# A weight piece's shift set ahead of two masks, and a product group that takes its operand half by half: two reorderings at the seam between an SSD scan and an ELU feed-forward layer

## The chip, the cores and the metric

The kernel runs on one core of a Trainium2 chip. The core has a matrix engine (TensorE, PE; its weight loads are listed apart as PEld), three elementwise engines (VectorE or DVE, ScalarE or ACT, GpSimd or POOL) and DMA queues, here issued by SyncE (SP). Each engine works through its own list of instructions in order; semaphores make one wait for another. The metric is the device time of one execution in microseconds; of several executions the median is given.

## The reference

Four batches of eight heads go through a chunked Mamba-2 state-space scan over 768 tokens (head width 32, state width 16). The result, one row of 256 numbers per token, goes through a feed-forward layer with an ELU in the middle.

```python
for c in range(nc):                      # chunks of 32 tokens
    la = log_a[:, :, sl]; cum = np.cumsum(la, axis=-1)
    L = np.exp(cum[:, :, :, None] - cum[:, :, None, :]) * causal
    M = np.einsum('bhin,bhjn->bhij', Cc, Bc) * L
    y_intra = np.einsum('bhij,bhjd->bhid', M, xc)
    y_inter = np.einsum('bhin,bhnd->bhid', Cc, state) * np.exp(cum)[..., None]
    y[:, :, sl] = y_intra + y_inter
    state = decay_full * state + np.sum(Bx, axis=2)
...
x = attn_out.transpose(0, 2, 1, 3).reshape(B * S, H * D)   # (3072, 256)
h = x @ w_in                                               # (3072, 2048)
g = np.where(h > 0.0, h, np.exp(np.minimum(h, 0.0)) - 1.0)
return (g @ w_out).astype(np.float32)                      # (3072, 256)
```

The two weight matrices come as float64.

## The kernel before

**Blocks.** The 3072 tokens are twelve blocks of 256 (`BLK`), in chunks of 64. Block `n` first goes through the scan, then through the layer. The scan of a block makes decays `L`, turned copies of B and C (`bt`, `ct`), C masked by the parity of the head (`ctm`, `mask_heads`, L477: two VectorE instructions for block one), C scaled by the running decay (`cts`, `turn_exp`, L458, written in place over `ct`), scores `ps_g` (`scores`, L582, from `bt` and `ctm`), weighted scores `M` (`weigh`, L591, on VectorE, four per block), state sums `ps_st` (`sums`, L612), states (`states`: `S_new` on VectorE, L627 and L629, and `Sx` on GpSimd, L634), and at last the output: `across` (L660, from the states and `cts`) and `inside` (L678, from `M`), both into `ps_y`. `inside` works in two halves `t`: heads zero to three, then heads four to seven. Each half is copied into `yT[n // 2][:, t]`; for block one the first half is copied by ScalarE (L695), the second by VectorE (L693), three copies each.

**Weights.** They arrive as float64 words in pieces, and are made float32 in five steps: `w_abs` (ScalarE, L205), `w_low` (ScalarE, L214, or VectorE, L218), `w_sign` and `w_high_a` (VectorE, L224 and L232), `w_high_b`, a shift with an exclusive or (VectorE, L239), and `w_sum`, an integer add (GpSimd, L249). Pieces 0 to 7 are the eight column groups of `w_in`, so piece 3 is the fourth; its magnitude lies in PSUM, so L232 and L239 of it read PSUM.

**First layer.** `l1(n, i)` multiplies block `n` by column group `i` into one PSUM buffer of 2 x 256 columns: for each of two column halves `j`, two products (`k`, the two halves of the 256 features, that is heads zero to three and four to seven, the `t` above). In the profile every float32 product is two passes, so a group of four products is eight. `parts=2` splits the 256 tokens into two halves, so that a group is eight products of 128 columns. The ELU follows with a lag: ScalarE (L730 and L737), then a join on VectorE (L738), which frees the buffer. There are seven rotating PSUM buffers (`p_a`), shared with the scores and the turned tiles.

**The order around the change** is written out by hand, one call after the other, and each engine keeps that order. In the stretch of block one, VectorE gets the first two steps of piece 3, the two masks of C, the shift of piece 3, the scaled C, an ELU join, two `M`, the states, two more `M`. TensorE has `l1(0, 2)`, the scores and sums of block one, `l1(0, 3)` (which reads piece 3), `across` and `inside` of block one, two small transposes, and then a loop of twelve groups (L1159), which starts with `l1(1, 0)` and `l1(1, 1)`, both with `parts=2`. From there on groups of the first layer, products of the second (L885) and scans of later blocks alternate; later blocks use split words and longer products (L832, L981).

Of the kernel before, what the change touches and what calls it, by code (L numbers as in the profile page):

```python
# [17 lines left out]
P = 128  # L18
Q = 64
BLK = 2 * P  # L20
# [7 lines left out]
def high_word_as_f32(word):  # L28

    return float(np.uint32(word).view(np.float32))  # L30
# [3 lines left out]
def kernel(  # L34
# [27 lines left out]
    nc = tc.nc  # L62
# [8 lines left out]
    KC, MC = DM // P, DF // P  # L71
# [19 lines left out]
    def psum(shape, name):  # L91
        return p_a.tile(shape, F32, tag="a", name=name)
# [7 lines left out]
    for k in range(4):  # L100
        (nc.scalar if k % 2 else nc.sync).dma_start(
            out=la0[BH * k:BH * (k + 1)],
# [61 lines left out]
    w_in = [None] * (DF // CW)  # L164
# [14 lines left out]
    def w_load(i, parts=1):  # L179
        if i < len(pieces):  # L180
            w_raw[i] = big([P, 2, 2 * CW], U32, "w64")
            for part in range(parts):
                cols = slice(2 * CW * part // parts, 2 * CW * (part + 1) // parts)
                nc.sync.dma_start(out=w_raw[i][:, :, cols], in_=pieces[i][1][:, :, cols])  # L184
# [37 lines left out]
    def w_sign(i, cols=slice(None)):  # L222
        w_parts_of(i)
        nc.vector.tensor_scalar(  # L224
            out=w_sgn[i][:, :, cols], in0=w_words(i)[1][:, :, cols], scalar1=0x80000000,
            scalar2=None, op0=ALU.bitwise_and)

    def w_high_a(i, cols=slice(None)):
        mag = w_abs_of.get((i, cols.start), w_mag[i])[:, :, cols]


        nc.vector.tensor_scalar(  # L232
            out=mag.bitcast(F32), in0=mag.bitcast(F32),
            scalar1=high_word_as_f32(0x38000000), scalar2=high_word_as_f32(0x47EFFFFF),
            op0=ALU.max, op1=ALU.min)

    def w_high_b(i, cols=slice(None), ks=slice(None)):
        mag, sgn = w_mag[i][:, ks, cols], w_sgn[i][:, ks, cols]
        nc.vector.scalar_tensor_tensor(  # L239
            out=mag, in0=w_abs_of.get((i, cols.start), w_mag[i])[:, ks, cols], scalar=3, in1=sgn,  # L240
            op0=ALU.logical_shift_left, op1=ALU.bitwise_xor)
# [47 lines left out]
    for v in range(2):  # L289
        nc.gpsimd.affine_select(  # L290
            out=low16[Q * v:Q * v + Q], in_=low16[Q * v:Q * v + Q], pattern=[[1, Q]],
# [5 lines left out]
        out=hmask, in_=hmask, pattern=[[-N, NH]], compare_op=ALU.is_ge, fill=0.0,  # L297
        base=0, channel_multiplier=1)
    nc.gpsimd.affine_select(
        out=hmask, in_=hmask, pattern=[[N, NH]], compare_op=ALU.is_ge, fill=0.0,  # L300
# [8 lines left out]
        out=minus, in0=ident, scalar1=-1.0, scalar2=None, op0=ALU.mult)  # L309
# [60 lines left out]
    def write_flat_exp():  # L370
        nc.sync.dma_start(out=flat_exp, in_=F[:, 1].rearrange("r u i -> r (u i)"))
# [15 lines left out]
    yT = {}  # L387
# [84 lines left out]
    def mask_heads(n, eng=nc.vector):  # L472
        s = st[n]
        s["ctm"] = att.tile([P, 2, 2, P], F32, tag="ctm", name="ctm")
        if eng is nc.vector:
            for k in range(2):
                eng.tensor_scalar(  # L477
                    out=s["ctm"][:, :, k], in0=s["ct"], scalar1=hmask2[:, k:k + 1],
                    scalar2=None, op0=ALU.mult)
            return  # L480
        eng.tensor_tensor(
            out=s["ctm"], in0=s["ct"].unsqueeze(2).to_broadcast([P, 2, 2, P]),
            in1=hmask2.unsqueeze(1).unsqueeze(3).to_broadcast([P, 2, 2, P]), op=ALU.mult)
# [74 lines left out]
    def decay_of(n, h):  # L558
        L, row = st[n]["L"], rows_of(n).start + NG * h
        for u in range(2):  # L560
            nc.scalar.activation(
                L[:, h, u], L[:, h, u], ACT.Exp, bias=ncum[:, u, row:row + 1])
        if h % 4 == 3:
            for v in range(2):
                part = L[Q * v:Q * v + Q, h - 3:h + 1]
                nc.gpsimd.affine_select(
                    out=part, in_=part, pattern=[[0, 4], [0, 2], [1, Q]],
                    compare_op=ALU.is_ge, fill=0.0, base=0, channel_multiplier=-1)
# [3 lines left out]
    def scores(*ns, pool=p_a, tag="a"):  # L572

        gs = [psum([P, len(ns), 2, 2, Q], "ps_g") for _ in range(3)]
        gs.append(pool.tile([P, len(ns), 2, 2, Q], F32, tag=tag, name="ps_g"))
        for at, n in enumerate(ns):
            s = st[n]
            for u in range(2):
                for v in range(2):
                    for q in range(4):  # L580
                        rows, toks = slice(32 * q, 32 * q + 32), slice(Q * v, Q * v + Q)
                        nc.tensor.matmul(  # L582
                            out=gs[q][toks, at, u], lhsT=s["bt"][rows, u, toks],
                            rhs=s["ctm"][rows, u, :, toks], start=True, stop=True,
                            tile_position=(32 * q, Q * v), skip_group_check=True)
            s["g"], s["M"] = [g[:, at] for g in gs], []

    def weigh(n, q):
        s = st[n]
        M = att.tile([P, 2, 2, Q], F32, tag="M", name="M", bufs=8)  # L590
        nc.vector.tensor_tensor(  # L591
            out=M, in0=s["g"][q],
            in1=s["L"][:, 2 * q:2 * q + 2].rearrange("p k u i -> p u k i"), op=ALU.mult)
        s["M"].append(M)
# [8 lines left out]
    def sums(*ns, pool=p_a, tag="a", parts=(None, None)):  # L603

        ps = [psum([P, len(ns), 2, 2 * D], "ps_st"),
              pool.tile([P, len(ns), 2, 2 * D], F32, tag=tag, name="ps_st")]
        for at, n in enumerate(ns):
            s = st[n]
            for u, v in chunks(n, parts[at] or whole):
                toks = slice(Q * v, Q * v + Q)  # L610
                for q in range(4):
                    nc.tensor.matmul(  # L612
                        out=ps[v][32 * q:32 * q + 32, at, u],
                        lhsT=s["sc"][toks, u, 2 * q:2 * q + 2].rearrange("p h n -> p (h n)"),
                        rhs=s["x"][toks, u, 2 * D * q:2 * D * (q + 1)], start=True, stop=True,
                        tile_position=(Q * v, 32 * q), skip_group_check=True)
            s["st"] = [p[:, at] for p in ps]
# [88 lines left out]
            g_of[n // 2, i] = big([P, 2, 2, BLK], F32, "g")  # L706
        return g_of[n // 2, i]

    def l1(n, i, parts=1):

        ps = psum([P, 2, BLK], "ps_h")
        for j in range(2):
            m = 2 * i + j
            for part in range(parts):
                toks = slice(part * BLK // parts, (part + 1) * BLK // parts)
                for k in range(KC):
                    nc.tensor.matmul(  # L717
                        out=ps[:, j, toks], lhsT=w_in[i][:, k, j * P:(j + 1) * P],
                        rhs=yT[n // 2][:, k, n % 2].rearrange("p u i -> p (u i)")[:, toks],
                        start=(k == 0), stop=(k == KC - 1))  # L720
        lag.append((n, i, ps))

    lag = []
# [308 lines left out]
    def w_take(i, low):  # L1032

        w_abs(i)
        w_low(i, low)
        w_sign(i)

    def w_give(i):

        w_high(i)  # L1040
        w_sum(i)
# [75 lines left out]
    w_low(3, nc.scalar)  # L1117
    w_sign(3)
    w_high_a(3)
    mask_heads(1)  # L1120
    w_high_b(3)
    write_flat_exp()
    load_bc(2)
    w_load(6)
# [34 lines left out]
    for s, (n, i) in enumerate((  # L1159
            (1, 0), (1, 1), (1, 2), (0, 4), (1, 3), (0, 5), (1, 4), (0, 6), (1, 5), (0, 7),  # L1160
            (1, 6), (1, 7))):
        l1(n, i, parts=2 if s < 2 else 1)
        if s < 8:
            decay_of(2, s)
        if s == 7:
            st[0] = kept
            scores(2)
            sums(2, 0, pool=p_o, tag="o", parts=(None, last))
            weigh(2, 0)
            weigh(2, 1)  # L1170
        if s % 2 == 1 and todo < 11:
            w_take(todo, nc.vector)
            w_give(todo)
            w_load(todo + 6)
            todo += 1
        if s in (1, 3):
            load_bc(3, us=(s // 2,))
        if s == 9:
            write_flat(0)
        if s == 4:  # L1180
            scaled(2, nc.gpsimd)
        if s == 5:
            turn(2)
            turn_exp(2)
        if s == 4:
            load_x(3)
            spread_exp(3)
        if s == 8:
            weigh(2, 2)
            weigh(2, 3)  # L1190
            states(0, last)
            st.pop(0)
            states(2)
        if s == 9:
            decay(3, 0)
            decay(3, 1)
        if s == 10:
            spread_cum(4)
            inside(across(2), 2)
        if len(lag) > 1:  # L1200
            elu()
# [23 lines left out]
    for j in range(2 * DIRECT):  # L1225
        n, i = 2 + j // DIRECT, j % DIRECT
# [47 lines left out]
    for j in range(8, 16):  # L1274
        i = j - 8
# [84 lines left out]
    for n in range(4, NP, 2):  # L1360
        m = n + 2 if n + 2 < NP else None
# [78 lines left out]
    n = NP - 2  # L1440
# [45 lines left out]
```

## Time and profile before

| | |
|---|---|
| median of 3 runs | 339.98 us (339.45 to 340.72) |
| profiled execution | 338.85 us |
| its span, first to last instruction | 337.1 us |
| busy: PE, DVE, ACT, POOL | 330.4, 286.7, 259.0, 214.2 us |
| share of PE in the chain that ended last | 92% |
| granted TensorE clock | 0.999 |

A row of the timeline gives the start in us from the beginning of the span, the duration, the engine, the line of the kernel, the operation, the tile written and those read, the shapes, and how many instructions are merged into the row (`x2`); in square brackets stands how long the engine had been idle before and what released it. A row of the table by stage gives the stage, its length, the busy time of PE, PEld, DVE, ACT and POOL with the instructions in brackets, the granted clock, and the DMA's share and rate. A row of waits gives who waited for whom, for how many us in all, how often, and the longest.

### The profile page before, as it was taken

The page shows a single profiled execution, that of the slowest core. Times are in us where ns is not written, and L with a number is a line of the kernel's source. Part 1 is how long each engine was busy: PE and PEld are TensorE (multiplying, and loading weights), DVE is VectorE, ACT ScalarE, POOL GpSimd, SP SyncE. Part 2 cuts the span into 40 slices and gives each one's busy share as a digit, 9 for nine tenths or more (in the row PEclk, how much of TensorE's full clock was granted, in tenths as well). Part 3 has the DMA queues.
Part 4 walks back from the last instruction along what each step waited for, and adds up shares of the span by engine and source line. Part 5 has one row for each costly group of instructions (what it writes and reads, how often), then busy time and mean ns, then how long its engine had stood idle before and what let it go on. Part 6 is the DMA issues. An engine that isn't in the chain of part 4 may idle for free.

```text
span 337.1 us, 9647 instructions
## 1 busy us (share of the span) xinstructions
PE 330.4 (98%) x3742; PEld 288.2 (85%) x3742; DVE 286.7 (85%) x511; ACT 259.0 (77%) x537; POOL 214.2 (64%) x242
## 2 busy tenths in 40 slices
PE   8899999999999999999999999999999999999995
PEld 5578888888888888888899988889889899999995
DVE  4998998889897889898989998989996978997942
ACT  5789989599857699857898866898867789897501
POOL 5454554648979396989489979388974355776000
PEclk9999999999999999999999999999999999999999
DMA  8889999553487388671769491669440762330101
GB/s 141 218 237 181 293 193 277 127 108 123 158 158 290 126 217 272 200 185 16 272 189 215 138 300 27 263 188 191 126 156 8 277 212 101 104 118 0 33 0 63
DMA packets 82956, 54.79 MB, mean 163 GB/s; under 512 B 59038, under 2 KB 68574, under 8 KB 82910
## 3 DMA queue, kind: packets, MB, share of 16 engines
q1 hardware_dynamic: 80734, 53.98, 57.4%
q8 instruction: 29, 0.48, 0.6%
q10 hardware_dynamic: 2176, 0.20, 0.5%
q14 instruction: 17, 0.14, 0.1%
HBM read 44.53 MB, written 9.63 MB: 161 GB/s over the span
## 4 chain that ended last, share of the span: by engine, by line
PE 92%; SPq 2%; DMA 2%; ACT 2%; DVE 1%; issue 0%; DVEq 0%; ACTq 0%
PE ps_o L981 24%; PE ps_h L832 20%; PE ps_o L885 12%; PE ps_h L717 11%; PE ps_w L832 10%; PE ps_both L981 6%; PE ps_y L678 3%; DMA w<-in_moe_w_in_dram 2%; PE ps_g L582 2%; PE ps_y L660 2%; PE ps_st L612 1%; PE ps_high L981 1%; SPq L156 1%; SPq L184 0%; ACT w_in L214 0%; SPq L124 0%
## 5 line engine op out<-in xcount | busy, mean ns | idle before, releaser
L899 POOL TENSOR_TENSOR g_words<-g_words,g_low 128x512 fp32r<-128x512 f32 x62 | 82.3, 1331 | 49.2 <-DVE g_low L923 25.8
L981 PE MATMUL ps_o<-o_words,g_words 128*128 128x256 f32 x448 | 83.4, 284 | 0.0
L981 PEld LDWEIGHTS ps_o<-o_words,g_words 128*128 128x128 f32 x448 | 72.9, 190 | 5.8 <-POOL g_words L899 0.8
L860 ACT ACTIVATE e<-ps_h 128x512 f32<-128x512 f32 x72 | 43.0, 597 | 35.1 <-DVE ps_h L848 35.1
L867 DVE SCALAR_TENSOR_TENSOR g<-e,ps_h 128x512 f32<-128x512 f32 x72 | 49.3, 684 | 19.0 <-ACT e L861 17.1
L981 PE MATMUL ps_o<-o_low,g_low 128*128 128x256 f32 x224 | 63.3, 283 | 0.0
L923 DVE SCALAR_TENSOR_TENSOR g_low<-g_words,g 128x512 fp32r<-128x512 f32 x72 | 63.3, 885 | 0.0
L848 DVE SCALAR_TENSOR_TENSOR ps_h<-ps_h,e 128x512 f32<-128x512 f32 x72 | 49.8, 691 | 2.7 <-ACT e L840 2.6
L832 PE MATMUL ps_w<-y_both,w_words 128*128 128x512 f32 x144 | 48.7, 419 | 0.0
L861 ACT ACTIVATE e<-e 128x512 f32<-128x512 f32 x72 | 45.5, 633 | 2.3
L717 PE MATMUL ps_h<-yT,w_in 128*128 128x256 f32 (+1 forms) x208 | 45.2, 367 | 1.6 <-ACT yT L695 1.0
L840 ACT ACTIVATE e<-ps_w 128x512 f32<-128x512 f32 x72 | 41.9, 582 | 5.4 <-PE ps_w L832 5.4
L885 PE MATMUL ps_o<-w_out,g 128*128 128x256 f32 x192 | 45.5, 380 | 0.0
L832 PE MATMUL ps_h<-y,w_words 128*128 128x512 f32 x144 | 45.3, 395 | 0.0
L832 PE MATMUL ps_h<-y,w 128*128 128x512 f32 x144 | 44.7, 391 | 0.0
L922 ACT ACTIVATE g_words<-g 128x512 fp32r<-128x512 f32 x72 | 43.6, 625 | 0.0
L981 PEld LDWEIGHTS ps_o<-o_low,g_low 128*128 128x128 f32 x224 | 42.7, 191 | 0.0
L717 PEld LDWEIGHTS ps_h<-yT,w_in 128*128 128x128 f32 x208 | 36.2, 190 | 7.5 <-POOL w_in L249 2.3
L885 PEld LDWEIGHTS ps_o<-w_out,g 128*128 128x128 f32 x192 | 36.1, 190 | 5.4
L832 PEld LDWEIGHTS ps_h<-y,w 128*128 128x128 f32 x144 | 27.0, 188 | 6.2
L832 PEld LDWEIGHTS ps_h<-y,w_words 128*128 128x128 f32 x144 | 26.6, 188 | 6.6 <-issue 0.7
L832 PEld LDWEIGHTS ps_w<-y_both,w_words 128*128 128x128 f32 x144 | 23.5, 191 | 2.0 <-ACT e L860 0.2
(132 smaller groups left out, 548.2 us busy)
## 6 DMA issues: line engine op xcount, KB each, us to landing
w_words<-w_kept SPq DMA_DIRECT2D x28, 512.0 KB
w<-w_kept SPq DMA_DIRECT2D x28, 256.0 KB
L<-flat SPq DMA_DIRECT2D x20, 256.0 KB
w<-in_moe_w_out_dram SPq DMA_DIRECT2D x8, 512.0 KB
w_kept<-w_words SPq DMA_DIRECT2D x8, 512.0 KB
w<-in_moe_w_in_dram SPq DMA_DIRECT2D x7, 512.0 KB
xr<-in_x_dram SPq DMA_DIRECT2D x24, 128.0 KB
out_dram<-eo SPq DMA_DIRECT2D x18, 128.0 KB
```

The costliest lines, as they stand in the source:

```text
L717: nc.tensor.matmul(out=ps[:, j, toks], lhsT=w_in[i][:, k, j * P:(j + 1) * P], rhs=yT[n // 2][:, k, n % 2].rearrange("p u i -> p (u i)")[:, ...
L832: nc.tensor.matmul(out=ps, lhsT=lhs[:, k], rhs=rhs[:, k], start=k == 0 and lhs is not w0, stop=k == KC - 1 and lhs is not w1)
L840: nc.scalar.activation(e, both, ACT.Copy, scale=WORD)
L848: nc.vector.scalar_tensor_tensor(out=high, in0=high, scalar=WORD - 1.0, in1=e, op0=ALU.mult, op1=ALU.add)
L860: nc.scalar.activation(e, high, ACT.Relu, scale=-1.0)
L861: nc.scalar.activation(e, e, ACT.Exp, scale=-1.0)
L867: nc.vector.scalar_tensor_tensor(out=g_tile(n, m // 2)[:, m % 2].rearrange("p b i -> p (b i)"), in0=e, scalar=1.0, in1=h, op0=ALU.subtract ...
L885: nc.tensor.matmul(out=o_of[n][:, ts], lhsT=g_of[n // 2, j][:, m % 2, n % 2, ts * P:(ts + 1) * P], rhs=w_out[j][:, m % 2], start=(m == 0 a ...
L899: nc.gpsimd.tensor_tensor(out=out, in0=in0, in1=in1, op=ALU.subtract)
L922: yield nc.scalar.activation(words[:, 0], g, ACT.Copy, scale=NEAR / WORD)
L923: yield nc.vector.scalar_tensor_tensor(out=low, in0=words[:, 0].bitcast(F32), scalar=WORD, in1=g, op0=ALU.mult, op1=ALU.subtract)
L981: nc.tensor.matmul(out=ps, lhsT=lhs, rhs=rhs, start=lhs is both_g and first > 0 or lhs is g1 and first > 1, stop=last and lhs is not g1, s ...
```

## The change

Two things move. First, the shift of piece 3 (`w_high_b(3)`) is issued ahead of `mask_heads(1)`, so that on VectorE it passes the two masks. Second, `l1` loses its split by tokens. The loop's first group, `l1(1, 0)`, now runs over the feature halves outside and the column halves inside: both column halves with heads zero to three, then both with heads four to seven, 256 tokens each; only its first product starts the PSUM buffer afresh. The second group, `l1(1, 1)`, becomes a group as all others, four products of 256 columns.

```diff
-    def l1(n, i, parts=1):
+    def l1(n, i, by_half=False):
         ps = psum([P, 2, BLK], "ps_h")
-        for j in range(2):
-            m = 2 * i + j
-            for part in range(parts):
-                toks = slice(part * BLK // parts, (part + 1) * BLK // parts)
-                for k in range(KC):
-                    nc.tensor.matmul(
-                        out=ps[:, j, toks], lhsT=w_in[i][:, k, j * P:(j + 1) * P],
-                        rhs=yT[n // 2][:, k, n % 2].rearrange("p u i -> p (u i)")[:, toks],
-                        start=(k == 0), stop=(k == KC - 1))
+        order = [(j, k) for j in range(2) for k in range(KC)]
+        if by_half:
+            order = [(j, k) for k in range(KC) for j in range(2)]
+        for at, (j, k) in enumerate(order):
+            nc.tensor.matmul(
+                out=ps[:, j], lhsT=w_in[i][:, k, j * P:(j + 1) * P],
+                rhs=yT[n // 2][:, k, n % 2].rearrange("p u i -> p (u i)"),
+                start=(at == 0 if by_half else k == 0), stop=(k == KC - 1),
+                skip_group_check=by_half)
         lag.append((n, i, ps))
...
     w_high_a(3)
+    w_high_b(3)
     mask_heads(1)
-    w_high_b(3)
     write_flat_exp()
...
-        l1(n, i, parts=2 if s < 2 else 1)
+        l1(n, i, by_half=s == 0)
```

## The prediction

> **What bounds the kernel now.** I read the page first, then the chain of waits, the table by stage, the waits inside the stage that the diff touches, and last the timeline of that stage engine by engine. Page, busy time and the chain that ended last:
>
> ```profile
> span 337.1 us, 9647 instructions
> PE 330.4 (98%) x3742; PEld 288.2 (85%) x3742; DVE 286.7 (85%) x511; ACT 259.0 (77%) x537; POOL 214.2 (64%) x242
> PE 92%; SPq 2%; DMA 2%; ACT 2%; DVE 1%; issue 0%; DVEq 0%; ACTq 0%
> ```
>
> TensorE (PE) is 98% busy and 92% of the chain. The table by stage shows where it is not full:
>
> ```profile
> 20.00:27.00 7.00, 6.45 (x172) 4.71 (x172) 6.52 (x19) 5.31 (x12) 2.50 (x5) 1.00 0.78 195
> 27.00:100.00 73.00, 73.00 (x801) 62.23 (x803) 64.69 (x129) 61.20 (x153) 45.70 (x60) 1.00 0.73 180
> 100.00:300.00 200.00, 199.81 (x2184) 176.59 (x2182) 176.85 (x290) 163.08 (x309) 146.78 (x142) 1.00 0.59 178
> ```
>
> After each stage's length comes PE's busy time: 6.45 of 7.00 us in the stage of the change, 73.00 of 73 and 199.81 of 200 behind it. So whatever moves the first product behind 27 us moves the end by the same amount, in either direction; nothing behind absorbs it. Both edits lie in that one stage. Its waits, and its timeline:
>
> ```profile
> PE ps_h L717 <- DVE M L591: 0.4, 1, 0.4
> PEld ps_h L717 <- DVE yT L693: 0.3, 1, 0.3
> ```
>
> ```profile
> 19.02 0.69 DVE L232 TENSOR_SCALAR ps_mag<-ps_mag 128x512 f32<-128x512 f32 x1
> 19.62 0.60 DVE L477 TENSOR_SCALAR ctm<-bct,hmask 128x256 f32<-128x256 f32 x2
> 20.14 0.68 DVE L239 SCALAR_TENSOR_TENSOR mag<-ps_mag,mag 128x512 uint32<-128x512 uint32 x1
> 20.74 0.41 DVE L458 TENSOR_TENSOR bct<-bct,ec 128x256 f32<-128x256 f32 x1
> 20.79 0.76 PE L582 MATMUL ps_g<-ctm,bct 32*64 32x128 f32 x32
> 20.96 1.33 POOL L249 TENSOR_TENSOR w_in<-mag,w_in 128x512 uint32<-128x512 uint32 x1 [1.39 <-DVE mag L239]
> 21.32 0.69 DVE L738 SCALAR_TENSOR_TENSOR g<-e,ps_h 128x512 f32<-128x512 f32 x1 [0.17 <-ACT e L737]
> 21.93 0.75 DVE L591 TENSOR_TENSOR M<-ps_g,L 128x256 f32<-128x256 f32 x2
> ```
>
> The reader is to see the order on VectorE (DVE): both masks, the shift of the fourth piece (L239), the scaled C (L458), the ELU join (L738), the first two M. GpSimd (POOL) sums the piece (L249) once the shift is done. The group l1(0, 3) starts at 22.35, when both its piece (20.96 + 1.33 = 22.29) and its PSUM buffer (first M, 21.93 + 0.42 = 22.35) have come: two releasers within 0.06 us.
>
> **Edit 1: the shift ahead of the masks.** No instruction is added or removed; on DVE the shift passes the two masks, no queue of DMAs is passed, and the rows on the other engines keep their order. Step by step:
>
> Masks before the shift now separate L232 from L239, which reads what L232 wrote. Next to each other they can't overlap. Unrelated neighbours overlap by 0.07 to 0.08 us (19.02 + 0.69 = 19.71 against 19.62); where the later one reads the earlier one's result the row is 16.25 + 0.42 = 16.67, next start 16.70, so 0.03. Shift: 19.74 to 20.42. First mask: 20.34, 0.34 long, to 20.68; the second issues at 20.60.
>
> The sum on POOL started 0.14 after the shift's end (20.82 to 20.96), so it now starts at 20.56 and lasts 1.28 us: to 21.84, 0.45 earlier. That gain is worth nothing by itself, because the M still frees the buffer at 22.35.
>
> But the sum now runs beside the second mask and L458; before, it began when both masks were done. What a POOL operation does to such DVE instructions, other stages show:
>
> ```profile
> 17.54 1.28 POOL L249 TENSOR_TENSOR w_in<-mag,w_in 128x512 uint32<-128x512 uint32 x1 [1.25 <-DVE mag L239]
> 17.98 1.12 DVE L224 TENSOR_SCALAR mag<-w 128x512 uint32<-128x512 uint32 x1
> 80.42 1.73 POOL L899 TENSOR_TENSOR w<-w_in,w_words 128x256 fp32r<-128x256 f32 x2
> 81.40 0.91 DVE L477 TENSOR_SCALAR ctm<-bct,hmask 128x256 f32<-128x256 f32 x1
> 82.11 0.71 POOL L566 TENSOR_SCALAR_AFFINE_SELECT L<-L 64x512 f32<-64x512 f32 x1
> 82.23 0.75 DVE L477 TENSOR_SCALAR ctm<-bct,hmask 128x256 f32<-128x256 f32 x1
> ```
>
> L224 is 0.42 us elsewhere; here it took 1.12 and ended 0.28 behind the sum. The same masks, of another block, took 0.91 and 0.75 instead of 0.34, and each ended 0.16 behind a POOL instruction (80.42 + 1.73 = 82.15, mask end 82.31; 82.82, mask end 82.98). DVE waits out the whole POOL instruction. PSUM readers don't: L232 kept 0.69 to 0.70 us beside sums.
>
> The price is bounded from both sides. None, if the second mask and L458 slip through: 0. Full, if the second mask waits: it ends at 21.84 + 0.15 = 21.99; L458 rewrites in place what the mask read, so it starts at 22.02 and ends at 22.43; L738 at 22.35 (its exponential is there since 21.29) to 23.04; first M 22.96 to 23.38; l1(0, 3) at 23.38 instead of 22.35: +1.03 us. The scores need both masks and go from 20.79 to 22.02; with the sums they last 1.16 us, to 23.18, inside that. Should the second mask win the 0.04 us race against the sum (20.60 against 20.56), L458 waits instead: its two inputs are in SBUF, and such a form (the words of w, 0.68 us alone) took 0.98 beside POOL in the row at 77.77. It then ends about 0.28 behind a sum that itself is put off by about 0.25 us, at 22.37, and l1(0, 3) starts near 23.32: +0.97. The race decides little. I take +1.03: the mask rows at 81.40 and 82.23 are the same instruction in the same shape, and in both the POOL instruction went first, at 82.11 with a lead of only 0.12 us.
>
> Here a page of the Trainium skill can be weighed. The first mask issues 0.22 us before the sum, as L458 did before (20.74 and 20.96), and that sum took 1.33 instead of 1.28 us. By SBUF — State Buffer, "Who interferes with whom", whichever issues first holds the shared ports for its whole instruction and the other fully blocks; then the sum would wait for the first mask's end (20.68, 0.12 us), and edit 1 would cost 1.15 instead of 1.03. The row of 1.33 shows 0.05 lost, so I stay with the rows.
>
> Later work of the stage moves as a whole: states, Sx, across and inside of block one hang on the same DVE order (Sx ended at 24.27 and across began at 24.27), so l1(1, 0) would start at 26.06 + 1.03 = 27.09.
>
> **Edit 2: l1(1, 0) by heads, whole tokens.** Before, the first products:
>
> ```profile
> 26.06 0.38 PE L717 MATMUL ps_h<-yT,w_in 128*128 128x128 f32 x1
> 26.28 0.28 PE L717 MATMUL ps_h<-yT,w_in 128*128 128x128 f32 x1
> 26.70 0.38 PE L717 MATMUL ps_h<-yT,w_in 128*128 128x128 f32 x1
> 30.15 0.38 PE L717 MATMUL ps_h<-yT,w_in 128*128 128x256 f32 x1
> ```
>
> A float32 product shows as two passes. Two passes on heads zero to three start at 26.06, then PE waits for the last DVE copy of heads four to seven (released 26.64), and groups (1, 0) and (1, 1) give way to the next at 30.15: 4.09 us for 32 passes of 128 columns. After: 16 passes of 256. A group of eight is 1.73 us in the chain (61.30 to 63.03), and 1.83 when it starts after a stop (22.35, second pass 22.67, then six more by 0.216 and the last one's own 0.216). So 1.83 + 1.73 = 3.56, a gain of 0.53 us. The cover: the first four passes last 0.32 + 3 x 0.216 = 0.97, to 27.03 on the old clock, and the copies are there at 26.64, 0.39 early. Were that cover gone, the stop would be back at up to 0.42. Of the gain about 0.11 is the halves themselves (32 x 0.1115 = 3.57 against 16 x 0.216 = 3.46). Behind it the fifth piece is ready at 28.78 and needed by (0, 4) only at 31.9: no new wait there, even 1 us later.
>
> **Sum.** +1.03 - 0.53 = +0.50 us. The profiled execution took 338.85 us for a span of 337.1, and would take 339.35; it lies 1.13 under the median shown, 339.98, which becomes 340.48. 0.5% (1.70 us) is about what a measurement of this kernel can tell from no change; this is 0.15%.
>
> **Rivals.** (a) No collision: the sum and the second mask don't get in each other's way. Then scores start near 21.0, done well before L591 needs them, l1(0, 3) stays at 22.35, and only edit 2 counts: 339.98 - 0.53 = 339.45. For it: which of POOL and mask goes first hangs on 0.04 us of estimate, and L224 at 12.88, issued 0.07 us ahead of a sum, kept its 0.42. Against: L458 must get through as well, and no row of the trace shows such a DVE instruction, issued behind a POOL instruction, ending before it. 0.15.
>
> (b) Edit 2 doesn't do what it says in time: the collision comes, and the copies of heads four to seven, which are behind more DVE work than the ScalarE copies, come so late that the wait is back. For it: DVE carries the whole delay; against: both halves of yT shift together, with 0.39 to spare. +1.03 - 0.11, about 340.9. 0.06.
>
> (c) The other side, clearly slower: the longer stops take PE's clock down. PE would rest from 20.86 to 22.02 and 0.2 us more before 23.38. If the granted clock halved from the stop to l1(1, 0) at 27.09, 6.2 us at half speed cost up to 3.1 more: 343.6. It decides from 2.4 us of half clock on (0.50 + 1.2 = 1.70). Against: a stop of 0.97 us ahead of 12.46 left the granted clock at 1.00 in every stage. By TensorE: Matmul & The Clock Gate, Part 1, the clock falls only after an idle window of about 3.4 us, which would exclude it; no run here shows such a window. 0.04.
>
> **How the numbers follow.** Forecast 0.72, (a) 0.15, (b) 0.06, (c) 0.04, unnamed 0.03. The prediction is 340.5. Single runs spread from 339.45 to 340.72, so a median may be off by 0.3: from (a) less 0.3, 339.1, to (b) with 0.4, 341.3. The forecast, (a) and (b) are all within 0.5%: same 0.93; (c) and part of the unnamed are slower, 0.05; faster 0.02, unnamed alone.
>
> **What would show it.** Right: in the changed profile the second mask takes about 1.4 us and ends just behind L249, L582 starts near 22.0, l1(0, 3) near 23.4, and the rows of l1(1, 0) follow each other without the stop at 26.28 to 26.70. Wrong: both masks at 0.34 and L458 at 0.41 (then (a)), a wait for DVE yT in front of the third product (then (b)), or a granted clock under 1.00 between 20 and 28 us (then (c)).

## The result, and the profile after

The changed kernel takes 342.57 us (median of nine executions, 341.39 to 345.15) against 339.59 us for the one before (nine, 338.94 to 340.72): ratio 1.0091, 95% interval 1.0067 to 1.0116. It is slower by 3.0 us, where 0.5 us was forecast and 341.3 us was the upper end of the range. The profiled execution took 342.11 us for a span of 340.4 us.

Page of the changed kernel, busy time and chain:

```profile
span 340.4 us, 9615 instructions
PE 330.6 (97%) x3726; PEld 287.5 (84%) x3726; DVE 288.0 (85%) x511; ACT 259.0 (76%) x537; POOL 214.6 (63%) x242
PE 92%; SPq 3%; DMA 2%; DVE 1%; issue 1%; DVEq 0%
```

PE has the same busy time in a span that is 3.3 us longer, and 16 entries fewer in each of its two rows. So the loss is made of stops. The table by stage, of the changed kernel, shows where (length of the stage, then PE's busy time):

```profile
20.00:27.00 7.00, 5.38 (x131) 3.86 (x130) 6.61 (x17) 4.32 (x9) 2.45 (x6) 1.00 0.87 208
100.00:155.00 55.00, 55.00 (x570) 46.93 (x570) 47.20 (x76) 43.54 (x83) 44.71 (x46) 1.00 0.68 209
155.00:162.00 7.00, 5.72 (x200) 5.10 (x199) 5.03 (x6) 4.67 (x10) 6.31 (x5) 1.00 0.11 16
```

There are two places: the stage of the change, and one at 155 to 162 us, 130 us behind it, where PE was busy for 6.81 us before. In the first, the collision of edit 1 came as described. Timeline of the changed kernel, VectorE and GpSimd, with the two masks also one by one:

```profile
20.19 0.69 DVE L239 SCALAR_TENSOR_TENSOR mag<-ps_mag,mag 128x512 uint32<-128x512 uint32 x1
20.79 0.34 DVE L477 TENSOR_SCALAR ctm<-bct,hmask 128x256 f32<-128x256 f32 x1
21.02 1.26 POOL L249 TENSOR_TENSOR w_in<-mag,w_in 128x512 uint32<-128x512 uint32 x1 [1.00 <-DVE mag L239]
21.05 1.38 DVE L477 TENSOR_SCALAR ctm<-bct,hmask 128x256 f32<-128x256 f32 x1
22.54 0.42 DVE L458 TENSOR_TENSOR bct<-bct,ec 128x256 f32<-128x256 f32 x1
22.58 0.70 PE L582 MATMUL ps_g<-ctm,bct 32*64 32x128 f32 x32 [1.27 <-DVE ctm L477]
```

The second mask is issued 0.03 us behind the sum, takes 1.38 us instead of 0.34 and ends at 22.43, 0.15 behind the sum's end. Then comes what the prediction had not: rows of PE for the output of block one and, later, of blocks four and five, in the changed kernel:

```profile
26.22 0.44 PE L678 MATMUL ps_y<-M,xr 64*32 64x64 f32 x28
27.34 0.60 PE L678 MATMUL ps_y<-M,xr 64*32 64x64 f32 x36 [0.68 <-issue]
158.16 1.29 PE L678 MATMUL ps_y<-M,xr 64*32 64x64 f32 x104
160.72 0.43 PE L678 MATMUL ps_y<-M,xr 64*32 64x64 f32 x24 [1.28 <-issue]
```

In the middle of a run of small products PE stands still, and the profile names no engine or DMA as releaser ("issue"). Before, the second of these places had 0.19 us, the first none:

```profile
157.68 0.65 PE L678 MATMUL ps_y<-M,xr 64*32 64x64 f32 x40 [0.19 <-issue]
```

Setting the two traces side by side, product by product, gives the delay of the changed kernel against before. It is +0.40 us ahead of the stage (the start-up differs by up to 1.5 us from one profile to the next, in unchanged code), +1.36 at l1(0, 3), +2.19 at l1(1, 0), +1.67 at the transposes behind the sixth group, +1.75 at 147 us, +2.82 behind the stop near 160 us, +3.16 at 248 us. So: collision +0.96, stop in block one +0.83 with what surrounds it, edit 2 -0.52, stop in blocks four and five +1.07, and about 0.3 in small pieces behind.

### The profile page after: what moved, and what is told of

It reads as the page before. It is cut to its first block, busy times and chain, and to the rows that moved or that the text cites. A ratio compares the mean times of both kernels' runs of the same rounds, so it can differ in the third digit from the quotient of the medians.

```text
span 340.4 us, 9615 instructions
## 1 busy us (share of the span) xinstructions
PE 330.6 (97%) x3726; PEld 287.5 (84%) x3726; DVE 288.0 (85%) x511; ACT 259.0 (76%) x537; POOL 214.6 (63%) x242
## 4 chain that ended last, share of the span: by engine, by line
PE 92%; SPq 3%; DMA 2%; DVE 1%; issue 1%; DVEq 0%
PE ps_o L981 24%; PE ps_h L832 20%; PE ps_o L885 12%; PE ps_h L716 11%; PE ps_w L832 10%; PE ps_both L981 6%; PE ps_y L678 3%; PE ps_g L582 2%; DMA w<-in_moe_w_in_dram 2%; PE ps_y L660 2%; PE ps_st L612 1%; SPq L140 1%; PE ps_high L981 1%; SPq L184 1%; SPq L156 1%
## 5 line engine op out<-in xcount | busy, mean ns | idle before, releaser
L832 PE MATMUL ps_w<-y_both,w_words 128*128 128x512 f32 x144 | 48.6, 419 | 0.0
L716 PE MATMUL ps_h<-yT,w_in 128*128 128x256 f32 x192 | 44.9, 383 | 1.2 <-ACT yT L695 1.0
L832 PE MATMUL ps_h<-y,w_words 128*128 128x512 f32 x144 | 45.3, 395 | 0.0
L832 PE MATMUL ps_h<-y,w 128*128 128x512 f32 x144 | 44.6, 391 | 0.0
L716 PEld LDWEIGHTS ps_h<-yT,w_in 128*128 128x128 f32 x192 | 35.6, 190 | 7.3 <-POOL w_in L249 2.1
L832 PEld LDWEIGHTS ps_h<-y,w_words 128*128 128x128 f32 x144 | 26.6, 188 | 6.8 <-issue 0.5
L832 PEld LDWEIGHTS ps_h<-y,w 128*128 128x128 f32 x144 | 27.0, 188 | 6.2
L832 PEld LDWEIGHTS ps_w<-y_both,w_words 128*128 128x128 f32 x144 | 23.6, 191 | 1.9 <-DVE y_both L816 0.2
```

Source lines behind the costliest of these rows:

```text
L716: nc.tensor.matmul(out=ps[:, j], lhsT=w_in[i][:, k, j * P:(j + 1) * P], rhs=yT[n // 2][:, k, n % 2].rearrange("p u i -> p (u i)"), start=( ...
L832: nc.tensor.matmul(out=ps, lhsT=lhs[:, k], rhs=rhs[:, k], start=k == 0 and lhs is not w0, stop=k == KC - 1 and lhs is not w1)
```

## Experiments: collision, or also the two stops, and where these come from

Each run below is set against executions of the kernel before in the same round, so that the time before reads 339.45 to 339.68 us. The ratio in brackets, with its 95% interval, is not quite that of the two medians (for edit 2 alone these give 1.0052, where the ratio is 1.0045), so a few tenths of a us between two runs are not to be read.

A theory had to explain stops without a releaser. The page lists a DMA queue of its own for instructions, here in the changed kernel:

```profile
q8 instruction: 29, 0.48, 0.6%
```

0.48 MB in 29 packets are 16,384 bytes each. Counting PE's entries in the trace in order (products, weight loads and what its sequencer handles alone; 7584 before, 7552 after), the two stops of the changed kernel fall at entries 961 and 4033, which lie exactly 12 x 256 apart, and the stop of before falls at 4033 too. So the theory ("code theory"): PE's list of instructions arrives in blocks of 256; PE stops at a border if it has run through a block faster than the next was fetched. Small products run through one in less than 2 us (entries 3777 to 4033 of the changed kernel pass in 1.64 us). A group in whole tokens has four products instead of eight; a float32 product is four entries, so edit 2 takes 32 entries out and moves all later borders. The rival ("delay theory"): the stops follow from the later start of everything, by new collisions of transfers.

The Trainium skill, Runtime: NRT & Kernel Launch, "Instruction fetch mechanics", describes such blocks of 16 KiB and 256 instructions, fetched while the one ahead is executed, and calls the cost mostly hidden. The 16,384 bytes and the distance of 256 agree. It is hidden at most borders here too (in the kernel before, the stop of 0.19 us is PE's only one behind 27 us), but not at all: at two borders PE of the changed kernel stops for 0.68 and 1.28 us.

### Each edit alone, and the count alone

Edit 1 alone:

```diff
     w_high_a(3)
+    w_high_b(3)
     mask_heads(1)
-    w_high_b(3)
```

> Edit 1 alone (shift of piece 3 ahead of the masks; products as before). Code theory: besides the collision on GpSimd's sum, the extra loss comes from blocks of PE's instruction list that arrive late; their borders lie where PE's instruction count puts them. Then this run, which keeps PE's count, loses the collision (+1.0 us at l1(0, 3)) and perhaps the stop inside block one's L678 (+0.7 to 0.9, because the block needed there is asked for only when the scores start, now beside the loads of block two), in all +1.0 to +2.0 us, and shows no stop near 157 to 161 us longer than the 0.19 us of before. Delay theory: everything beyond the collision follows from the later start of the rest, whatever the count: +3.0 (result) + 0.5 (gain of edit 2 missing) = +3.5 us, with a stop of 1.2 us or more near 160 us.

Measured: 341.05 us against 339.68, +1.4 us (ratio 1.0046, 1.0028 to 1.0065). The second mask took 1.39 us. PE stopped in block one, and the place near 157 us had no stop:

```profile
27.53 0.60 PE L678 MATMUL ps_y<-M,xr 64*32 64x64 f32 x36 [0.60 <-issue]
```

The delay theory's +3.5 us fails, although everything behind started late.

Edit 2 alone:

```diff
-        l1(n, i, parts=2 if s < 2 else 1)
+        l1(n, i, by_half=s == 0)
```

> Edit 2 alone (masks first, as before; l1(1, 0) by heads, whole tokens in both groups). Code theory: -0.5 us at the group behind l1(1, 1), then a stop of 1.0 to 1.5 us inside L678 near 157 to 160 us and some 0.2 to 0.3 us near 245 us, since eight products fewer move the borders of the instruction blocks: in all +0.4 to +1.0 us. Delay theory: no late start, so no stop: -0.5 us (-0.3 to -0.7). No collision: both masks at 0.34 us.

Measured: 341.45 us against 339.68, +1.8 us (1.0045, 1.0025 to 1.0064), more than either theory said; the direction is that of the code theory. Both masks took 0.34 us, nothing was late, and still:

```profile
156.19 1.29 PE L678 MATMUL ps_y<-M,xr 64*32 64x64 f32 x104
159.12 0.43 PE L678 MATMUL ps_y<-M,xr 64*32 64x64 f32 x24 [1.64 <-issue]
```

In this profile the granted clock fell behind the stop. Table by stage; the granted clock is the third figure from the end:

```profile
158.00:160.00 2.00, 0.88 (x26) 0.74 (x26) 0.42 (x1) 0.16 (x1) 2.00 (x2) 1.00 0.30 45
161.00:163.00 2.00, 2.00 (x9) 1.83 (x8) 1.78 (x3) 1.87 (x4) 0.00 (x0) 0.50 0.99 346
164.00:166.00 2.00, 2.00 (x16) 1.86 (x15) 2.00 (x4) 1.51 (x3) 0.08 (x1) 1.00 0.57 125
```

The trace has it at 0.50 for 3.41 us from 160.37 on. There the delay against before grew by another 1.5 us, which the expectation had not priced.

Count alone, no other order:

```diff
-        l1(n, i, parts=2 if s < 2 else 1)
+        l1(n, i)
```

> The kernel before with whole tokens in the first two groups, old order inside a group: eight products fewer for PE and nothing else. Code theory: the stop near 157 to 160 us grows from 0.19 to 1.0 to 1.5 us, and the time by +0.8 to +1.4 us, although PE has 0.1 us less work. Delay theory: 0 to -0.1 us, stop unchanged.

Measured: 341.30 us against 339.68, +1.6 us (1.0039, 1.0014 to 1.0065), a little above the code theory's range. PE has less to do, no step has moved, and the kernel is slower:

```profile
156.08 1.29 PE L678 MATMUL ps_y<-M,xr 64*32 64x64 f32 x104
158.77 0.43 PE L678 MATMUL ps_y<-M,xr 64*32 64x64 f32 x24 [1.40 <-issue]
```

The heads' order alone, with the count of before:

```diff
-        for j in range(2):
-            for part in range(parts):
-                for k in range(KC):
+        order = [(j, part, k) for j in range(2) for part in range(parts) for k in range(KC)]
+        if by_half:
+            order = [(j, part, k) for k in range(KC) for j in range(2) for part in range(parts)]
...
+        l1(n, i, parts=2 if s < 2 else 1, by_half=s == 0)
```

> The kernel before with l1(1, 0) by heads zero to three, then four to seven, tokens still in halves: PE's count of instructions is that of before. Both theories: the wait for the copies of heads four to seven goes, -0.3 to -0.45 us. Code theory adds that the stop near 157 us stays at 0.1 to 0.4 us; if it grew to over 1 us here, with the count unchanged, that theory falls.

Measured: 339.29 us against 339.68, -0.4 us as both theories said, though the interval of the ratio (0.9972 to 1.0016) doesn't tell it from no change. There is no stop near 157 us.

By their medians, edits 1 and 2 alone add up: 1.4 + 1.8 = 3.2 us, and the change cost 3.0.

### The changed kernel with its count refilled, and other counts

The changed kernel, eight products more ahead of block one:

```diff
-    l1(0, 1)
+    l1(0, 1, parts=2)
...
-    l1(0, 2)
+    l1(0, 2, parts=2)
```

> The changed kernel, with the groups l1(0, 1) and l1(0, 2) in halves of tokens instead: eight products more, so that PE's count behind l1(1, 1) is that of before, and the border of the block that block one's L678 needs lies 32 records earlier, ahead of the scores' wait. Code theory: both stops (0.68 us near 27 us, 1.28 us near 160 us) go to under 0.4 us, and what is left is what was forecast, collision less gain: +0.3 to +0.7 us against before. If the loss came from the later start itself, it stays at +2 to +3 us.

Measured: 340.14 us against 339.45, +0.69 us (1.0012, 0.9988 to 1.0036). The collision is there, both stops are gone:

```profile
21.61 1.64 DVE L477 TENSOR_SCALAR ctm<-bct,hmask 128x256 f32<-128x256 f32 x2
23.39 0.70 PE L582 MATMUL ps_g<-ctm,bct 32*64 32x128 f32 x32 [1.21 <-DVE ctm L477]
27.04 0.80 PE L678 MATMUL ps_y<-M,xr 64*32 64x64 f32 x57
158.42 1.54 PE L678 MATMUL ps_y<-M,xr 64*32 64x64 f32 x128
```

The same order of work, with the same late start, takes about what the prediction's sum gave: +0.5 us lies inside the interval, +2 us doesn't. This run decides between the theories.

Edit 1 alone, with `l1(0, 2, parts=2)`:

> Edit 1 alone, with l1(0, 2) in halves of tokens: the border ahead of the scores is passed 16 records earlier. Code theory: the stop of 0.60 us near 27.5 us goes, the collision stays: +0.7 to +1.1 us (edit 1 alone gave +1.4). Rival, that the stop comes from the loads of block two standing in PE's way in any case: the stop stays, +1.4 us.

Measured: 341.43 us against 339.45, +2.0 us (1.0039, 1.0011 to 1.0066): the time is a miss. The stop in block one did go (its L678 runs through), but at another border a new one came:

```profile
105.39 1.46 PE L885 MATMUL ps_o<-w_out,g 128*128 128x256 f32 x6
107.92 0.59 PE L885 MATMUL ps_o<-w_out,g 128*128 128x256 f32 x2 [1.07 <-issue]
```

Edit 2 alone, halves in the third and fourth group instead of the first two:

```diff
-        l1(n, i, by_half=s == 0)
+        l1(n, i, parts=2 if s in (2, 3) else 1, by_half=s == 0)
```

> Edit 2 alone, but the third and fourth group of the loop in halves of tokens, so that PE's count is that of before behind them. Code theory: the stop near 158 us is back under 0.4 us, and the time is -0.3 to -0.6 us, although the first two groups take whole tokens as in the change. If whole tokens in those two groups were themselves the cause, it is +1.8 us again, as with edit 2 alone.

Measured: 339.09 us against 339.45, -0.36 us (0.9975, 0.9949 to 1.0002), no stop near 157 us. Whole tokens in the first two groups do no harm; the count did.

The kernel before with four groups in halves (`parts=2 if s < 4 else 1`):

> The kernel before, with four groups of the loop in halves instead of two: eight products more. Code theory: the border moves the other way, the stop of 0.19 us near 157 us goes to nothing, and the time is -0.1 to +0.2 us (0.1 us of work more, 0.2 of stop less), other stops unknown. Rival, that any other count is worse: +1 us or more.

Measured: 343.92 us against 339.45, +4.5 us (1.0116, 1.0069 to 1.0163): a bad miss in the time. The rival's price came. The stop near 157 us is gone as expected, and a longer one came at an earlier border, entry 3009:

```profile
103.87 0.63 PE L832 MATMUL ps_h<-y,w_words 128*128 128x512 f32 x2
107.37 0.61 PE L832 MATMUL ps_h<-y,w 128*128 128x512 f32 x2 [2.88 <-issue]
```

"Other stops unknown" stood in the expectation, and a price should have stood beside it. Every other count tried (32 entries fewer, 16 or 32 more than before) had a stop of over 1 us at some border; whether another count would do better was not tried. All long stops together, with the packets of the instruction queue from the trace:

| kernel | entry at which PE stops | packet of the next block, us | PE goes on | behind the packet's end | stop |
|---|---|---|---|---|---|
| before | 4033 | 155.36 to 156.30 | 157.68 | 1.37 | 0.19 |
| changed | 961 | 24.39 to 26.02 | 27.34 | 1.32 | 0.68 |
| changed | 4033 | 158.29 to 159.17 | 160.72 | 1.56 | 1.28 |
| edit 1 alone | 961 | 25.26 to 26.19 | 27.53 | 1.35 | 0.60 |
| edit 2 alone | 4033 | 156.71 to 157.65 | 159.12 | 1.47 | 1.64 |
| count alone | 4033 | 156.33 to 157.31 | 158.77 | 1.46 | 1.40 |
| edit 1, l1(0, 2) halved | 3009 | 105.51 to 106.58 | 107.92 | 1.33 | 1.07 |
| four groups halved | 3009 | 105.03 to 106.06 | 107.37 | 1.31 | 2.88 |

Shorter stops at such borders stood in three more places: 0.27 us at entry 3009 with edit 1 alone, and 0.31 and 0.29 us at entry 961 in the last two runs below. 961, 3009 and 4033 lie 8 and 4 times 256 apart; of twelve traces with 28 borders each, not one border was passed earlier than 1.28 us behind the end of its packet.

Why eight products decide: the packet for the block behind entry 4033 starts 0.27 to 1.06 us ahead of `across` in the seven traces with the count of before (155.36 against 155.63 in the kernel before), and 0.89 to 1.28 us behind it in the three with 32 entries fewer (158.29 against 157.40 in the changed kernel). PE comes to the border at nearly the same point of the work in both: 1.66 us behind the start of `across` before, 1.83 in the changed kernel. So the fetch has about 1 us less. Which entry asks for the packet isn't shown. Entry 3777, one block ahead, lies within `across` in both kernels, 0.06 and 0.20 us behind its start, and can't explain the shift. A request some entries earlier would: entries 3728 to 3760 are the last 16 long passes ahead of `across` before and take 2.0 us; with 32 entries fewer they are its first 16 small ones and take 0.14 us. This is argued from the two traces, and no run tried it.

### The collision alone

Edit 1 alone, with piece 3's low part, and so its sum, later:

```diff
     turn_b(1)
-    w_low(3, nc.scalar)
...
     scaled(1, nc.gpsimd)
-    w_sum(3)
     turn_exp(1)
     l1(0, 2)
     elu()
+    w_low(3, nc.scalar)
+    w_sum(3)
```

> Edit 1 alone, but piece 3's low part is made later on ScalarE, behind the ELU's exponential of group (0, 1), so that GpSimd's sum of the piece starts about 1 us behind the shift, when masks and scaled C are done. Collision theory: both masks take 0.34 us again, the scores start near the end of l1(0, 2) (less than 0.3 us of stop instead of 1.2), and l1(0, 3) waits for the late piece alone: 0.3 to 0.6 us later than before, total 0 to +0.7 us. Rival, that the shift's new place delays the masks whatever GpSimd does: the second mask still takes over 1 us and the scores stop PE for 1 us or more; with the late piece, total +1.5 us or more.

Measured: 339.95 us against 339.63, +0.32 us (1.0008, 0.9991 to 1.0025). With the sum out of the way both masks, in the same place behind the shift, are short:

```profile
21.11 0.61 DVE L477 TENSOR_SCALAR ctm<-bct,hmask 128x256 f32<-128x256 f32 x2
22.50 1.28 POOL L249 TENSOR_TENSOR w_in<-mag,w_in 128x512 uint32<-128x512 uint32 x1 [2.16 <-ACT w_in L214]
```

So the masks are slow because of GpSimd's sum, not because of their place. `l1(0, 3)` came 0.38 us later than before, counted from the start of `l1(0, 2)`, as expected of the late piece.

The version with halves in the third and fourth group, once more:

> The version with edit 2 and its count refilled by halves in the third and fourth group, once more, for a closer figure against before: -0.2 to -0.6 us on both theories of the stops, since it has neither a collision nor a moved border.

Measured: 339.30 us against 339.63, -0.33 us (0.9986, 0.9966 to 1.0006). Together with -0.36 it is the fastest version tried; it beats the changed kernel clearly, and the one before by about the 0.1% that its single edit is worth, which neither interval tells from nothing. A stop of 0.29 us at entry 961 stood in its profile, so that border is close for all versions.

## Why the prediction was wrong

Every sign that the prediction named for being right came (L582 at 22.58 and `l1(0, 3)` at 23.71, 0.40 us of each from the start-up), and the time still missed: all of these signs lay in the stage of the change, and more than half of the loss that it left out lay behind that stage.

**Edit 1's price, +1.03 us: right.** +0.96 at l1(0, 3) in the profile. The second mask waited out the sum, L458, the join and the first M followed, and the piece that was ready 0.5 us earlier was worth nothing. The sum, issued 0.11 us before the first mask's end, took 1.26 us and did not wait, so the dearer price of 1.15 us that the prediction weighed didn't come.

**Edit 2's gain, -0.53 us: right.** Groups (1, 0) and (1, 1) took 3.56 us as worked out (28.26 to 31.82) instead of 4.09, without the stop for the copies. Rows of the changed kernel, whose L716 is the L717 of before:

```profile
28.26 0.92 PE L716 MATMUL ps_h<-yT,w_in 128*128 128x256 f32 x3
31.17 1.03 PE L716 MATMUL ps_h<-yT,w_in 128*128 128x256 f32 x4
```

**"Later work of the stage moves as a whole": wrong.** `across` moved by +1.33 us and `l1(1, 0)` by +2.19, and between them stands the stop of 0.68 us inside block one's L678. The border one block ahead of that stop, entry 705, lies at the first entries of the scores, for which PE now waited. The packet started 1.8 us behind the scores' first product instead of 1.0 (24.39 against 22.58, 21.80 against 20.79), and took 1.63 us instead of 0.98, on a stretch in which the loads of block two were issued. With 32 and 16 entries more ahead of the scores, in the refilled kernel and in edit 1 with `l1(0, 2)` halved, the packet started 1.5 and 2.2 us ahead of them, and the stop was gone. That the loads make the packet late was not tried, and stays open.

**"So whatever moves the first product behind 27 us moves the end by the same amount": wrong, and this failed by most.** It holds for the work, but edit 2 was costed as PE's time only. That it takes 32 entries out of PE's list, and so shifts every border behind it, was no term of the sum. It cost 1.07 us near 160 us in the profile, and +1.6 us by the median of the run that changes the count alone. Part of that median is the clock: the six of its twelve executions with a mean granted clock of 0.998 or more have a median of 340.3 us, +0.6; the six at 0.994 to 0.995 have one of 342.4. The trace of before had the clue: 0.19 us of "issue" in L678 at 157.68, the only stop of PE behind 27 us.

**The range's upper end: wrong for the same reason.** The rivals held other prices for the same work, but none for the instruction list. **Rival (c)**, a lower clock, had a part in some executions, though not in the stage that it named: in the profile of edit 2 alone the clock was halved for 3.41 us behind the stop near 159 us, with no stop of PE over 1.64 us. By the Trainium skill, TensorE: Matmul & The Clock Gate, Part 1, the clock falls after an idle window of about 3.4 us, which would have excluded this; the measurement decides. Of the nine executions of the changed kernel, four had a mean granted clock of 0.993 to 0.995 and took 343.1 to 345.2 us; the five at 0.999 to 1.0 took 341.4 to 342.6. Over all runs, a mean clock of 0.995 or less goes with the longest stops: 19 of 37 executions of the four versions with a stop of 1.28 us or more in their trace (changed, edit 2 alone, count alone, four groups halved) had it, 6 of 82 of the other seven, and 13 of 85 of the kernel before in the rounds of the experiments. Since it occurs there as well, the stop isn't its only cause, and what decides between executions of one kernel isn't shown.

## What to carry to other kernels

Where PE is full, count its instructions as well as its time: a shorter list can be slower, because it moves the borders of the fetched blocks against the work. Here a block of small products passed in 1.64 us, and the packet of the next took 0.88 us or more and another 1.28 us or more until PE went on. A stop "by issue" inside a run of like instructions, a multiple of 256 entries away from another, is the sign, and splitting or joining a few products elsewhere moves it, though it can bring a stop at another border. And a reordering that lets GpSimd start earlier is to be checked for what VectorE then does beside it.

## What the runs showed of the hardware

The instruction queue brought 29 packets of 16,384 bytes, one for each block of 256 entries of PE's list; PE went on 1.28 us or more behind a packet's end at each of 336 borders, and stops at such borders reached 2.88 us, also ahead of large products (L832 at 107.37), when the block in front held a run of small ones. The next packet started from 4.3 us ahead of PE's coming to a border to 8.0 us behind it; what sets this stays open. A VectorE mask issued 0.03 us behind a GpSimd sum took 1.38 instead of 0.34 us and ended 0.15 us behind it.
